# Moving output transposes and a ranking step within a hand-written instruction order (gated linear attention, then a two-level mixture of experts)

## The chip, the cores and the metric

The kernel runs on one core of one Trainium2 chip. The metric is device time in microseconds of one execution; the figure for the kernel before is the median of three runs. An engine name stands for its instruction queue: PE (TensorE, matrix products and transposes), PEld (its weight loads), DVE (VectorE), ACT (ScalarE), POOL (GpSimd), SP (SyncE, which issues most of the transfers).

## The reference

First comes a gated recurrence over 768 steps for 4 batches and 8 heads of 48 channels, then a mixture of 16 experts in 4 groups, with one expert for each of the 3072 tokens.

```python
f = 1.0 / (1.0 + np.exp(-f_logit))
for t in range(S):
    state = f[:, :, t, :, None] * state + np.einsum('bhd,bhe->bhde', k[:, :, t], v[:, :, t])
    y[:, :, t] = np.einsum('bhd,bhde->bhe', q[:, :, t], state)
x = y.transpose(0, 2, 1, 3).reshape(B * S, H * D)          # 3072 x 384
g_idx = argmax(x @ w_group);  e_idx = argmax(x @ w_expert[g_idx])
out = softmax weight of group * softmax weight of expert * (relu(x @ w1[g, e]) @ w2[g, e])
```

All data are 32-bit floats.

## The kernel before

**Two stages.** The first stage computes the recurrence, the routing logits and each token's rank within its expert. It writes the rows x to a table in DRAM (`x_dram`), with the token's weight and number beside each row. The second stage goes over the experts, gathers each expert's rows from that table, multiplies by w1 and w2, and scatters the result to the output.

**Units.** The first stage works in 12 units: six chunks `c` of 128 tokens by two pairs `s` of batches. Unit `i` has c = i // 2 and s = i % 2. The steps of a unit are generators, and each mention of a letter in a hand-written list advances one of them by one piece. PE, DVE, ACT and SP execute exactly in the order in which the lists issue. POOL alone is ordered by the scheduler.

The letters that matter here, with their lines:

- `l` (load) issues q, k, v and f; `c` (`bounded`, L597) bounds f on DVE; `g` (`gated`) takes an exponential and a logarithm on ACT (L607, L610), two decay products `cs` on PE (L616), and two exponentials of each, `eq` and `kh`, on ACT (L617, L618). It also sends the last row of `eq` to a small tile `ends`, through POOL for units up to 9 (L623).
- `m` (`multiplied`) forms `qh` and `kh` on DVE (L636, L639); `t` (`turned`) transposes them on PE (L650), and ACT copies them to `Tq` and `Tk` (L651).
- `b` (`decayed`) transposes `ends` into the decays of a whole chunk (`gt`, L659), which ACT copies (L660). It acts in odd units only.
- `s` (`scored`) computes scores `ap` on PE (L689, or L704 in the first and last three units) and masks them to `am` on DVE (L692, L707).
- `z` copies half of v for the other rows (ACT, L667).
- `w` (`weighed`) makes the products of the state with q (L742) and then the products for slots, that is masked scores times v (L754, L746), and ACT copies the result to `xT` (L757).
- `n` (`stated`) makes the products `ds` for the new state (L722) and then the state on DVE: sum and product with the decays (L727, L728).
- `d` (`done`) makes the logits: `lT` on PE (L770), the copy `lgT` on ACT (L772), then the transpose `lg` (L775) and a sum on DVE (L776).
- `x` (`listed`) turns the outputs back to rows: eight transposes `x_ps` on PE (L795) and three copies on ACT (L797, L800). Rows of units 0 to 7 are kept in SBUF and sent by SP later, four units at a time (`o`, L810, in units 8 and 9); later units send theirs at the third piece of `x` (L803).
- `r` advances the routing of a finished chunk by one of eight pieces. These are: maxima (L197 to L208, two pieces); rank products `rk` on PE (L213, L215) and an exponential on ACT (L216); ranks and counts on DVE (L221 to L224); tables of positions (`ln`, `val`, L230 to L243, two pieces); the weights, with the write of `meta` to DRAM through POOL (L246 to L256); the table products `tb` on PE (L261) and their sum on DVE (L266). For chunk 3 the fourth piece also ranks the experts and writes the numbers of the two most used ones to `who` (L282 to L300).

A number behind a letter shifts the unit: `x-1` is the previous unit's. The list `EVEN` serves units 4 and 6, `ODD` serves units 3, 5 and 7, and `ORDERS` has lists of its own for units 8 (`NU - 4`) to 12.

**Buffers.** Seven PSUM banks with one tag are handed out to whichever result comes next; a bank is free when its last reader is done. `xT`, `Tq` and `Tk` have two buffers each, `am` has three.

Of the kernel before, what the change touches and what calls it, by code (L numbers as in the profile page):

```python
# [23 lines left out]
def kernel(  # L24
# [374 lines left out]
    def fetch(pool, rows, n, top=N, late=False):  # L399

        w = {"n": n, "pool": pool, "early": top < N, "late": late, "blocks": [(j, min(P, n - j * P)) for j in range((n + P - 1) // P)]}
        w["x"] = pool.tile([P, len(w["blocks"]), RW], FP32, tag="xg", bufs=2 if pool is ep else 6, name="xg")
        for j, m in w["blocks"]:
            nc.gpsimd.indirect_dma_start(out=w["x"][:, j, :], out_offset=None, in_=x_dram[0:1 + top, :], in_offset=bass.IndirectOffsetOnAxis(ap=rows[:, j:j + 1], axis=0))  # L404
        return w
# [124 lines left out]
    with ExitStack() as fast:  # L530
# [31 lines left out]
        NU = len(units)  # L562
# [270 lines left out]
        def advance(gens):  # L833
# [10 lines left out]
            t1 t1 t1 t1 b1 c2 g2 g2 s1 s1 s1 s1 p d0 g2 g2 n0 n1 w1 w1 m2 m2 l4 n1  # L844
            d0 x1 x1 t2 t2 t2 t2 c3 g3 g3 x1 s2 s2 s2 s2 w2 g3 g3 d1 w2 n2 m3 m3 c4 g4 g4""".split()
        BEGUN = 3
        EVEN = "l+2 d-2 n-1 r r r x-1 x-1 t t t t g+1 g+1 x-1 r z s s w s s c+2 d-1 g+2 w g+2 n m+1 m+1".split()
        ODD = "l+2 d-2 r r x-1 x-1 t t t t b n-1 g+1 g+1 x-1 r z s s w s s c+2 d-1 g+2 w g+2 n m+1 m+1 r n".split()
        ORDERS = {
            NU - 4: "l+2 o d-2 n-1 r r r x-1 x-1 t t t t g+1 g+1 x-1 r z s s w s s c+2 d-1 g+2 w g+2 n m+1 m+1".split(),  # L850
            NU - 3: "l+2 o d-2 r r x-1 x-1 t t t t b n-1 r g+1 g+1 x-1 r s s s s c+2 w d-1 g+2 w g+2 n m+1 m+1 r n".split(),
            NU - 2: "d-2 r x-1 x-1 r t t t t g+1 g+1 r 1 x-1 s s s s w d-1 w n m+1 m+1 2 3".split(),
            NU - 1: "d-2 r r n-1 x-1 x-1 t t t t r x-1 r s s s s 4 w b d-1 w r r".split(),
            NU: "d-2 r e d-1 x-1 x-1 d-1 x-1 r r r e e r e r r e r r e r e r r e e e e e".split(),
# [3 lines left out]
        def step(nm, i):  # L858
            if nm == "r":
                advance(routes)  # L860
            elif nm == "e":
                next(first[0], None)
            elif nm == "p":
                next(pad)
            elif nm == "o":
                send_kept(i - (NU - 4))
            elif nm in "1234":
                load_next(*((0, 1), (1, 1), (0, 2), (1, 2))[int(nm) - 1])
            elif nm == "h":
                next(turning)  # L870
            elif 0 <= i < NU:
                if nm == "l":

                    load(i, ("k", "qh"))
                    if i + 1 < NU:
                        load(i + 1, ("f",))
                    load(i, ("v",))
                    return
                if (nm, i) not in steps_of:
                    steps_of[nm, i] = STAGES[nm](i)  # L880
                next(steps_of[nm, i], None)
# [14 lines left out]
        for i in range(BEGUN, NU + 1):  # L896
            if i == BEGUN:
                nc.sync.dma_start(out=x_dram[0:1, 0:DM].rearrange("o (h d) -> o h d", d=D), in_=blank[:, 0:D].unsqueeze(1).broadcast_to((1, H, D)))
                nc.sync.dma_start(out=x_dram[0:1, DM:RW], in_=blank[:, D:D + 2])
            for tok in ORDERS.get(i, ODD if i % 2 else EVEN):  # L900
                step(tok[0], i + int(tok[1:] or 0))
# [62 lines left out]
    for n in range(GE - 1):  # L964
        w = ws[n]
# [105 lines left out]
    with tc.If(more > 0), ExitStack() as late:  # L1071
# [5 lines left out]
        with tc.For_i(0, last, 1) as i:  # L1077
# [14 lines left out]
            w = fetch(ep, row, P, late=True)  # L1092
# [32 lines left out]
```

## Time and profile before

| what | value |
|---|---|
| time before, median of 3 runs (lowest, highest) | 412.93 us (411.81, 413.04) |
| the profiled execution: its time | 417.84 us |
| the profiled execution: its span | 416.0 us |
| granted TensorE clock | 0.994 |
| busy PE / DVE / ACT / POOL | 404.0 / 264.3 / 162.2 / 85.7 us |
| units 3 to 8, from the first cs in unit 3 to the first cs in unit 9 | 40.69 to 103.31 us |
| first weights of the experts issued by SP | 118.23 us |
| second stage runs on PE without pauses | from 164.3 us |

Times inside the span are counted from its start. The chain that ended last is a list of pieces in order of time; each piece is what the next one waited for. "issue" is time in which an engine waited for nothing that the profile shows. A timeline row gives start, duration, engine, line, operation, shapes and count; a bracket at its end names the idle time in front of it and what ended it.

### The profile page before, as it was taken

How to read it: one execution, taken by the hardware profiler on the slowest of the kernel's cores; microseconds unless marked ns; L12 is line 12 of the kernel's file. 1: busy time of each engine (PE TensorE's matmuls, PEld its weight loads, DVE VectorE, ACT ScalarE, POOL GpSimd, SP SyncE). 2: the span in 40 equal slices, each digit the busy share in tenths (PEclk: the TensorE clock that was granted, in tenths of full speed). 3: DMA queues.
4: the chain of work that ended last, by engine and by line, in shares of the span. 5: the costliest groups of instructions: out<-in, count | busy, mean ns of one | idle time of the engine just before them, and what ended most of it. 6: DMA issues, size and time to landing. Idle time of an engine off the chain costs nothing.

```text
span 416.0 us, 10268 instructions
## 1 busy us (share of the span) xinstructions
PE 404.0 (97%) x4143; PEld 371.9 (89%) x4143; DVE 264.3 (64%) x783; ACT 162.2 (39%) x365; POOL 85.7 (21%) x132
## 2 busy tenths in 40 slices
PE   8999999999999997999999999999999999999994
PEld 3888888888888966989999999999999999999992
DVE  6666878787998702440799767485595595584230
ACT  6777878887664211211223122222231232232220
POOL 5000010101040174001041221311321230120230
PEclk9999999999999999999999999999999999999999
DMA  9999987879869499855729467586495596485010
GB/s 191 208 216 197 201 179 147 164 159 289 244 225 378 163 337 345 318 179 184 271 84 335 137 245 265 164 315 208 170 348 169 217 352 200 173 318 162 28 48 24
DMA packets 132146, 88.99 MB, mean 214 GB/s; under 512 B 102582, under 2 KB 122748, under 8 KB 132090
## 3 DMA queue, kind: packets, MB, share of 16 engines
q1 hardware_dynamic: 125666, 75.50, 60.6%
q0 software_dynamic: 5792, 11.92, 9.5%
q10 hardware_dynamic: 632, 0.83, 0.6%
q8 instruction: 35, 0.57, 0.6%
q14 instruction: 21, 0.17, 0.1%
HBM read 78.71 MB, written 9.83 MB: 213 GB/s over the span
## 4 chain that ended last, share of the span: by engine, by line
PE 48%; issue 30%; DMA 9%; POOL 6%; DVE 3%; POOLq 1%; another core or an unknown queue 1%; ACT 1%; SPq 0%; ACTq 0%; DVEq 0%
PE hp L450 12%; PE yo L486 6%; DMA out_dram<-yt,xg 6%; PE yo L471 4%; PE cs L616 4%; POOL out_dram L461 4%; PE ap L704 3%; PE y L746 3%; POOL xg L404 2%; PE x_ps L795 2%; PE tr_q L650 2%; PE tr_k L650 2%; PE y L742 2%; PE ap L689 2%; PE y L754 2%
## 5 line engine op out<-in xcount | busy, mean ns | idle before, releaser
L450 PE MATMUL hp<-xe,w 128*128 128x128 f32 (+14 forms) x864 | 141.3, 323 | 2.6 <-issue 1.8
L450 PEld LDWEIGHTS hp<-xe,w 128*128 128x128 f32 x864 | 137.4, 192 | 4.5 <-issue 2.4
L486 PE MATMUL yo<-h,w 128*128 128x230 f32 (+13 forms) x672 | 115.8, 333 | 0.0
L433 DVE STREAM_TRANSPOSE yr<-yT 32x192 f32<-32x192 f32 (+1 forms) x208 | 70.5, 339 | 70.5 <-ACT yT L487 67.9
L486 PEld LDWEIGHTS yo<-h,w 128*128 128x128 f32 x672 | 113.7, 190 | 0.2
L451 ACT ACTIVATE h<-hp 128x256 f32<-128x256 f32 (+14 forms) x72 | 34.2, 478 | 109.1 <-PE hp L450 100.2
L426 DVE STREAM_TRANSPOSE xe<-xg 32x192 f32<-32x192 f32 (+1 forms) x208 | 69.6, 335 | 8.7 <-PE hp L450 5.8
L461 POOL DMA_INDIRECT out_dram<-yt,xg x32 | 34.5, 1078 | 156.1 <-ACT yt L458 150.5
L487 ACT COPY yT<-yo 128x230 f32<-128x230 f32 (+13 forms) x42 | 13.5, 325 | 80.5 <-PE yo L486 80.5
L404 POOL DMA_INDIRECT xg<-x_dram,rows_p x30 | 29.6, 986 | 51.1 <-DMA out_dram<-yt,xg 25.7
L471 PE MATMUL yo<-w,h 128*128 128x384 f32 x64 | 21.3, 486 | 0.0
L707 DVE TENSOR_TENSOR am<-ap,tri 128x512 f32<-128x512 f32 x24 | 15.1, 688 | 7.3 <-PE ap L704 7.3
L616 PE MATMUL cs<-ld_f,tri 128*128 128x384 f32 x48 | 18.5, 505 | 0.5 <-POOL blank L177 0.3
L471 PEld LDWEIGHTS yo<-w,h 128*128 128x128 f32 x64 | 11.9, 190 | 7.4
L458 ACT ACTIVATE yt<-yr,xg 128x384 f32<-128x384 f32 (+13 forms) x26 | 14.4, 604 | 5.4 <-DVE yr L433 5.4
L623 POOL DMA_DIRECT2D ends<-eq x10 | 5.4, 542 | 52.2 <-ACT eq L617 52.2
L692 DVE TENSOR_TENSOR am<-ap,seen 128x384 f32<-128x384 f32 x24 | 12.2, 551 | 5.5 <-PE ap L689 5.5
L757 ACT COPY xT<-y 128x512 f32<-128x512 f32 x24 | 13.4, 587 | 5.0 <-PE y L746 4.4
L651 ACT COPY Tk<-tr_k 128x512 f32<-128x512 f32 x24 | 15.2, 636 | 0.0
L651 ACT COPY Tq<-tr_q 128x512 f32<-128x512 f32 x24 | 15.0, 625 | 0.4 <-PE tr_q L650 0.3
L441 DVE COPY xe<-xg_ps 128x384 f32<-128x384 f32 (+1 forms) x4 | 2.1, 535 | 20.5 <-remote 9.7
L650 PE MATMUL tr_q<-ident,qh 128*128 128x128 f32 x96 | 14.5, 274 | 0.5 <-issue 0.5
(187 smaller groups left out, 448.4 us busy)
## 6 DMA issues: line engine op xcount, KB each, us to landing
w<-in_moe_w_dram SPq DMA_DIRECT2D x34, 1536.0 KB, 7.2
qh<-in_q_dram SPq DMA_DIRECT2D x12, 384.0 KB, 6.1
ld_k<-in_k_dram SPq DMA_DIRECT2D x12, 384.0 KB, 4.4
v<-in_v_dram SPq DMA_DIRECT2D x12, 384.0 KB, 5.4
ld_f<-in_f_logit_dram SPq DMA_DIRECT2D x11, 384.0 KB, 5.5
x_dram<-x_kept SPq DMA_DIRECT2D x2, 1536.0 KB
x_dram<-x POOLq DMA_DIRECT2D x2, 384.0 KB
x_dram<-x ACTq DMA_DIRECT2D x2, 384.0 KB, 7.4
```

What stands on the lines that cost most here:

```text
L404: nc.gpsimd.indirect_dma_start(out=w["x"][:, j, :], out_offset=None, in_=x_dram[0:1 + top, :], in_offset=bass.IndirectOffsetOnAxis(ap=rows ...
L426: squares(w, lambda n, k_, rk, g, rg: nc.vector.transpose(out=xT[rg, 0:n, k_], in_=x[rk, 0:n, g]))
L433: squares(w, lambda n, k_, rk, g, rg: nc.vector.transpose(out=y[rk, 0:n, g], in_=yT[rg, 0:n, k_]))
L450: nc.tensor.matmul(hp[:, o, :], lhsT=w1[:, ko, (f + o) * P:(f + o + 1) * P], rhs=w["xT"][:, ko, :], start=(ko == 0), stop=(ko == KO - 1))
L451: nc.scalar.activation(h[:, f:f + 2, :], hp, AF.Relu)
L461: sent = nc.gpsimd.indirect_dma_start(out=out, out_offset=bass.IndirectOffsetOnAxis(ap=w["x"][0:m, j, DM + 1:RW].bitcast(U32), axis=0), in ...
L471: nc.tensor.matmul(yp, lhsT=w["h"][:, fo, :], rhs=w2[:, fo, :], start=(fo == 0), stop=(fo == FO - 1))
L486: nc.tensor.matmul(yp, lhsT=w2[:, fo, m * P:(m + 1) * P], rhs=w["h"][:, fo, :], start=(fo == 0), stop=(fo == FO - 1))
L616: nc.tensor.matmul(cs.rearrange("t h d -> t (h d)"), lhsT=tri, rhs=nl[:, b], start=True, stop=True)
L650: nc.tensor.transpose(out=pt[:, a, :], in_=w[nm + "h"][:, b, 2 * a:2 * a + 2, :].rearrange("t r d -> t (r d)"), identity=ident)
L651: nc.scalar.copy(w["T" + nm][:, b], pt)
L707: nc.vector.tensor_tensor(am[:, r], ap[r], tri.unsqueeze(1).broadcast_to((P, HP, P)), OP.mult)
```

## The change

Only the lists of order change, for units 3 to 9.

In units 3 to 8 the pieces `x-1` (outputs of the previous unit turned to rows) move from the place around the transposes `t` to a place behind the logits `d-1`, and with them goes the piece `r` that stood behind them. All of this now stands in front of the second piece of `w`, the products for slots. The bound `c+2` follows it. In odd units that `r` is the rank products, in even units the table products and their sum.

In unit 9 the outputs stay where they are. There, the pieces `b n-1` (decays, and the new state on DVE) move from the place in front of the rank products to behind the piece of the ranking.

```diff
-        EVEN = "l+2 d-2 n-1 r r r x-1 x-1 t t t t g+1 g+1 x-1 r z s s w s s c+2 d-1 g+2 w g+2 n m+1 m+1".split()
-        ODD = "l+2 d-2 r r x-1 x-1 t t t t b n-1 g+1 g+1 x-1 r z s s w s s c+2 d-1 g+2 w g+2 n m+1 m+1 r n".split()
+        EVEN = "l+2 d-2 n-1 r r r t t t t g+1 g+1 z s s w s s d-1 x-1 x-1 x-1 r c+2 g+2 w g+2 n m+1 m+1".split()
+        ODD = "l+2 d-2 r r t t t t b n-1 g+1 g+1 z s s w s s d-1 x-1 x-1 x-1 r c+2 g+2 w g+2 n m+1 m+1 r n".split()
         ORDERS = {
-            NU - 4: "l+2 o d-2 n-1 r r r x-1 x-1 t t t t g+1 g+1 x-1 r z s s w s s c+2 d-1 g+2 w g+2 n m+1 m+1".split(),
-            NU - 3: "l+2 o d-2 r r x-1 x-1 t t t t b n-1 r g+1 g+1 x-1 r s s s s c+2 w d-1 g+2 w g+2 n m+1 m+1 r n".split(),
+            NU - 4: "l+2 o d-2 n-1 r r r t t t t g+1 g+1 z s s w s s d-1 x-1 x-1 x-1 r c+2 g+2 w g+2 n m+1 m+1".split(),
+            NU - 3: "l+2 o d-2 r r x-1 x-1 t t t t r g+1 g+1 x-1 r b n-1 s s s s c+2 w d-1 g+2 w g+2 n m+1 m+1 r n".split(),
```

## The prediction

> **What bounds the kernel now.** I read the page's first part, then the stages one by one.
>
> ```profile
> PE 404.0 (97%) x4143; PEld 371.9 (89%) x4143; DVE 264.3 (64%) x783; ACT 162.2 (39%) x365; POOL 85.7 (21%) x132
> ```
>
> TensorE bounds the span. Its ends are modelled, so the 97% hides short waits. The change touches units 3 to 9, which lie between 38 and 112 us. The table by stretches, cut at the first decay product (cs) of each unit, gives two rows of interest: span of the stretch, then busy time of PE, PEld, DVE, ACT, POOL, clock, DMA share, GB/s.
>
> ```profile
> 71.66:81.88 10.22, 10.21 (x244) 8.61 (x242) 8.73 (x26) 8.41 (x19) 1.30 (x2) 1.00 0.81 162
> 91.79:103.31 11.52, 10.48 (x249) 8.84 (x248) 8.90 (x26) 9.33 (x22) 2.04 (x3) 1.00 1.15 277
> ```
>
> A usual unit is PE-full at 9.9 to 10.2 us; DVE and ACT have 1.3 to 1.8 us of slack. The stretch into unit 9 is 11.52 us. The chain that ended last says why:
>
> ```profile
> 94.37 0.17 DVE meta L254
> 94.54 0.14 DVE table L266
> 94.68 0.43 issue
> 95.11 0.78 POOL x_dram L256
> 95.89 7.01 DMA ends<-eq
> 102.90 0.14 issue
> 103.03 0.20 PE gt L659
> ```
>
> On POOL the 4 KB transfer of the decays (ends) stands behind the routing's write of meta; it starts at 95.89 and lands 7.01 us later, and PE's transpose gt waits. Behind gt on PE stand the rank products and cs; behind it on DVE stand the state's product, the ranking of the early experts and the masks of unit 9. The DVE timeline (start, duration) shows the second:
>
> ```profile
> 101.21 0.55 DVE L727 TENSOR_TENSOR st<-st,ds 128x384 f32<-128x384 f32 x1
> 103.47 0.56 DVE L728 TENSOR_TENSOR st<-st,decays 128x384 f32<-128x384 f32 x1 [1.72 <-ACT decays L660]
> 103.95 0.22 DVE L221 TENSOR_TENSOR pick<-rk,run 128x64 f32<-128x64 f32 x1
> 106.85 2.46 DVE L707 TENSOR_TENSOR am<-ap,tri 128x512 f32<-128x512 f32 x4
> ```
>
> From 103.47 DVE has no idle time until 125.3. In units 9 and 10 it is as full as PE.
>
> The third place is smaller: in each unit the products for slots (y L754) start 0.57 us (lT) plus about 0.2 us after the scores, and reach the second mask before DVE has finished it. Unit 4, mask on DVE, then PE:
>
> ```profile
> 54.78 1.02 DVE L692 TENSOR_TENSOR am<-ap,seen 128x384 f32<-128x384 f32 x2 [0.41 <-PE ap L689]
> ...
> 55.61 0.28 PE L754 MATMUL y<-am,other 128*48 128x64 f32 x4
> 55.72 0.39 PE L754 MATMUL y<-am,v 128*48 128x64 f32 x3
> 55.86 0.26 PE L754 MATMUL y<-am,other 128*48 128x64 f32 x1
> ```
>
> Groups of four start every 0.11 us; the fifth, the first on the second mask, stretches to 55.86, just after the mask ends at 55.80. About 0.1 us is lost.
>
> [...] ends was ready when eq ended at 94.0, yet POOL issued it at 95.89, right behind x_dram. [...] Here the 4 KB took 7.01 us, with 1.5 MB of kept rows sent from 94.15; the trace's value is used. [...] Seven banks turn here, so a moved transpose also moves who waits for which bank.
>
> **The change part by part.** No instruction is added or removed. By the two built programs' orders, eight x_ps transposes per unit (0.87 us of PE) go behind lT, then the rank or table products (rk, tb), then the slots. On ACT the three copies to x_kept go between lgT and the exponential of f. On DVE the table's sum goes behind the masks. SP's order is unchanged; the kept rows are sent where they were, long after the copies. On POOL, in three chunks, ends goes in front of meta.
>
> 1. *gt of unit 9.* Before: from the last four tr_k (101.41) to cs (103.31), 1.90 us. Without gt it is 0.44 (the interval 91.35 to 91.79 in unit 8) + 0.12 for rk = 0.56. gt itself moves behind cs and keeps 0.14. PE gains 1.90 - 0.56 - 0.14 = 1.2 us. Can gt wait there? ends issues about 1.9 us earlier (94.0); even with 7.0 us it lands at 101.0, and PE asks at 101.97 + 1.54 = 103.5. No.
>
> But DVE keeps part. rk starts at 101.87; pick follows 0.33 us later (as at 134.28 and 134.61), at 102.2. Pick to masks is 106.85 - 103.95 = 2.90, so 105.1; then the state's two operations, 0.58 + 0.48: masks at 106.2, 0.65 earlier. PE would reach the slots at 103.65 (ap) + 1.99 + 1.03 + 0.57 = 107.25 and finds the first pair only at 106.2 + 1.25 = 107.45, the second at 108.65. So the stage ends about 0.7 us earlier, not 1.2. ACT now makes decays behind the issue of the next ends, near 105.2; the state's second operation comes at 105.7. The names of the early experts come with DVE, so the weight loads (118.23) start some 0.6 us earlier too.
>
> 2. *Slots.* With 0.87 + 0.2 us more PE work between scores and slots, the second mask is ready: 0.1 us in each of six units, 0.6.
>
> 3. *tb.* cs to tb is 1.46 us (71.50 to 72.96), cs to rk 1.39: 0.07 of waiting for val, three times, 0.2. At its new place val is old.
>
> 4. *gt in units 5 and 7.* tr_k to cs is 0.69 against 0.44 without gt. gt costs 0.14; about 0.1 each is the wait for a bank that DVE frees (0.5 us in three waits in the list). The new bank comes from ACT: 0.2.
>
> 5. *Cover given up.* The x_ps transposes stood between lg and tr_q and gave time to DVE and ACT. tr_k needs kh: DVE in an even unit now ends it at scores + 1.0 (mask) + wait for tb; counted from the unit's start that is 9.9 us, and PE asks 0.44 after the unit's end at 10.0. Slack 0.5. The scores need ACT's four copies: PE takes ds 0.85 + lg 0.25 + tr 1.75 + cs 1.45 = 4.3 us from the end of the slots; ACT takes xT 0.96 + logarithm 0.75 + 1.43 + 0.67 = 3.8. Slack 0.5. In front of xT, ACT now has lgT, the x copies (0.92), in odd units dl (0.27), and the exponential (0.75 to start of the next): it is ready 2.6 us after lT, PE ends the slots after 0.87 + 0.2 + 1.7 = 2.8. I cost it at nothing; bounds are 0 and 0.4 us a unit, 2.4 in all. Below nothing is excluded, since the gains are already in 2 to 4.
>
> Steps 2 to 4 give 1.0; with slacks this thin I take 0.7 of it. Sum: 0.7 + 0.7 = 1.4 us. Behind unit 9, PE has 0.2 to 1 us pauses only up to 164, and these hang on the same chain (ranking, meta at 139.51, gathers from 144.72), so they move along; from 164 on PE runs without a break, so the 1.4 us reaches the end. The profiled run, 417.84 us with a span of 416.0, would become 416.4 and 414.6. It lies 1.2% over the median of 412.93; by the same ratio the median becomes 411.5.
>
> **Rivals.**
>
> *The whole stall comes back.* If DVE's chain in unit 9 is no limit (PE's gaps there are only 0.2 us), step 1 gives 1.2, steps 2 to 4 give 1.0; a 0.53 us pause with no releaser at 56.5 may go too, if it hangs on order. 2.2 to 2.7 us: 410.2 to 410.7. For it: PE is the bound in the page. Against: DVE without idle time from 103.47 to 125.3.
>
> *Nothing much arrives.* The pauses of 0.1 us are pipeline effects that stay, and DVE's 0.65 is eaten by a later landing, for instance the gathers at 144.72 whose transfer has its own load. Gain under 0.5: 412.6. [...] Against: the 1.2 us stall is a plain one.
>
> *Slower: ACT becomes the bound of the units.* At its new place in front of the exponential the x copies push xT, logarithm and T copies back, and the scores wait. Until 0.5 us of lateness PE loses nothing; beyond it each unit pays the excess. At 0.73 us late six units pay 1.4 and the gain is gone; at 0.95 us the time is 1.2 us over before, 414.1. For it: slack of xT is only 0.2 us, and DVE's table sum, held by tb, now stands in front of f's bound, which the exponential waits for. Against: ACT was busy 8.4 us of 10.1, and the copies fall into its waits for lT (1.1 us) and f (0.7 us).
>
> **How the numbers follow.** About 0.3%, 1.24 us here, is what tells a change from none; below 411.7 is faster. Likeliest case 0.46, its own range 410.9 to 412.2, two thirds of it faster. Whole stall 0.22, faster. Nothing 0.18, same. Slower 0.14. Faster 0.31 + 0.22 = 0.53, same 0.15 + 0.18 = 0.33, slower 0.14. The range from 409.9 to 413.6 takes in the first two rivals and the edge of the third.
>
> **What would show it.** Right: gt of unit 9 without a wait for ends; ends in front of x_dram on POOL; stretches of 9.9 to 10.1 us; slots without the pause; masks of unit 9 starting 4.9 us after the end of ohe (5.55 before), with y L746 waiting for DVE. Wrong: ap L689 waiting for ACT Tk, or tr_k for DVE kh, in the six units; idle time of ACT's exponential behind table L266; PE pauses between 104 and 134 that grow by what unit 9 gave.

## The result and the profile after

| | before | changed |
|---|---|---|
| median (lowest, highest), 6 runs each, same chip | 412.49 us (411.81, 413.04) | 410.78 us (410.61, 411.04) |
| ratio, 95% interval | | 0.9961, 0.9948 to 0.9974 |
| profiled execution: time, span | 417.84, 416.0 us | 410.61, 408.8 us |

The change makes the kernel 1.7 us faster (1.1 to 2.1 by the interval). Two later sets on other chips gave 0.9977 (0.9967 to 0.9987) and 0.9967 (0.9960 to 0.9975). The prediction was 411.5 us against a median of 412.93, a ratio of 0.9965. The measured 410.78 lies between the range given to the likeliest case (from 410.9) and that of the rival in which the whole stall comes back (up to 410.7), so the time alone doesn't choose between them; the traces do.

The two profiled spans differ by 7.2 us, and that is not the change. The profile of before has pauses on PE from 158 to 164 us, where the experts' layers begin, and a clock of 0.50 behind them, from 164.9 to 168.3 us; the profile after has neither. At the last rank products of the first stage (`rk` L213), in front of that place, the traces stand at 134.28 and 132.54 us: 1.74 us apart, as the medians are. I compare the traces up to there.

The page's first part after the change:

```profile
PE 401.3 (98%) x4143; PEld 369.6 (90%) x4143; DVE 264.9 (65%) x783; ACT 162.9 (40%) x365; POOL 86.0 (21%) x132
```

The busy time of DVE, ACT and POOL is what it was: only waits have moved. The table by stretches, cut at the first decay product (`cs`) of units 6, 7, 8 and 9 (span of the stretch, then busy PE, PEld, DVE, ACT, POOL, clock, DMA share, GB/s):

```profile
69.92:80.03 10.11, 10.11 (x244) 8.57 (x242) 8.64 (x27) 8.65 (x20) 1.51 (x3) 1.00 0.73 143
80.03:90.00 9.97, 9.97 (x243) 8.64 (x243) 7.68 (x20) 8.38 (x21) 0.51 (x1) 1.00 0.88 177
90.00:100.87 10.87, 10.87 (x256) 9.51 (x255) 8.67 (x26) 9.42 (x23) 2.23 (x4) 1.00 0.99 253
```

The stretch into unit 9 was 11.52 us and is 10.87; its PE column now equals its span. `gt` has moved out of this stretch, behind `cs`, and its row on PE has no wait in front of it:

```profile
102.34 0.23 PE L659 MATMUL gt<-ident,ends 16*128 16x16 f32 x1
```

POOL's timeline shows why the transfer is earlier:

```profile
92.54 0.52 POOL L623 DMA_DIRECT2D ends<-eq  x1 [9.50 <-ACT eq L617]
93.05 0.20 POOL L255 COPY meta<-token 128x4 int32<-128x4 int32 x1
93.57 0.79 POOL L256 DMA_DIRECT2D x_dram<-meta  x1 [0.31 <-POOL meta L255]
```

`ends` goes ahead of `meta`, directly behind ACT's `eq`, at 92.54 instead of 95.89. The prediction had 94.0, the end of `eq` before; `eq` itself now ends at 92.25, since the outputs no longer stand in front of it on PE. It also goes 0.48 us ahead of the kept rows (SP issues them at 93.02; before, at 94.15, 1.74 us ahead of `ends`), and lands in 3.9 us instead of 7.01. PE asks for it at 102.34, about 5.9 us after it has landed.

What limits unit 9 now is in the chain of work that ended last, in the stretch from 85 to 112 us (start, length, what):

```profile
100.90 0.03 PE rk L213
100.93 0.10 PE rk L215 x4
101.06 0.24 DVE pick L221
...
103.89 0.15 DVE who L300
104.04 0.47 DVE st L727
104.51 0.03 issue
104.56 0.04 issue
104.60 0.56 DVE st L728
105.16 2.41 DVE am L707 x4
107.57 0.04 issue
107.61 1.09 PE y L746 x16
```

Between the rank products and the second half of the products for slots, everything on the path is on DVE. In the chain of before the same stretch was the transfer (7.01) and PE.

The slots of unit 4, whose rows of before had a gap at the second mask (PE timeline):

```profile
53.72 0.40 PE L770 MATMUL lT<-xT,gw 128*32 128x128 f32 x8
54.05 1.09 PE L795 MATMUL x_ps<-ident,xT 128*128 128x128 f32 x8
54.98 0.28 PE L261 MATMUL tb<-val,ln 128*128 128x64 bf16 x4
55.19 0.32 PE L754 MATMUL y<-am,v 128*48 128x64 f32 x4
...
55.67 0.28 PE L754 MATMUL y<-am,v 128*48 128x64 f32 x4
```

The fifth group keeps the pace. What the rows also show is the price: `x_ps` to the next product is 0.93 us here (54.05 to 54.98) and was 0.87 in front of `tr_q`.

**A ledger of starts.** PE's ends are modelled, so I work with the differences of starts from one kind of product to the next, from one `lg` to the next. (The eight `x_ps` in the rows above last 1.09 us by their modelled ends, and 0.93 from their start to that of `tb`.) Those of one kind, with the same neighbours, agree within 0.02 us over units and runs, save for pauses of up to 0.7 us that come in `y` L754 or `ds` in some units of some runs, with no releaser. Without these:

| | before | changed |
|---|---|---|
| unit with rank products, `lg` to `lg` | 10.23 | 10.22 |
| `cs` to scores, with `rk` in it before | 1.39 + 0.21 | 1.49 |
| `x_ps` | 0.87 | 0.93 |
| `rk` at its new place | | 0.21 |
| `y` L754 | 1.79 | 1.62 |
| unit with table products, `lg` to `lg` | 10.07 | 9.86 |
| `cs` to scores, with `tb` in it before | 1.48 + 0.22 | 1.39 |
| `x_ps` | 0.87 | 0.93 |
| `tb` at its new place | | 0.21 |
| `y` L754 | 1.79 | 1.62 |
| unit 9, `lg` to `lg` | 12.05 (in a second profile of before: 11.66) | 11.41 |
| unit 10, `lg` to `lg` | 9.82 | 9.83 |

A pair of units gains 0.22 us, three pairs 0.66; unit 9 gains 0.64 or 0.25, by how long `gt` waited. In the first two profiles 0.66 + 0.64 = 1.3, and the rest of 1.74 is pauses: 0.6 in unit 4 of before, 0.12 in unit 5 after.

### The profile page after: what moved, and what is told of

Same layout as the page of the kernel before. It is cut to its first block, busy times and chain, and to the rows that moved or that the text cites. A ratio compares the mean times of both kernels' runs of the same rounds, so it can differ in the third digit from the quotient of the medians.

```text
span 408.8 us, 10274 instructions
## 1 busy us (share of the span) xinstructions
PE 401.3 (98%) x4143; PEld 369.6 (90%) x4143; DVE 264.9 (65%) x783; ACT 162.9 (40%) x365; POOL 86.0 (21%) x132
## 3 DMA queue, kind: packets, MB, share of 16 engines
HBM read 78.71 MB, written 9.83 MB: 217 GB/s over the span
## 4 chain that ended last, share of the span: by engine, by line
PE 52%; issue 30%; DMA 8%; POOL 6%; DVE 2%; POOLq 1%; ACT 0%; SPq 0%; DVEq 0%
PE hp L450 12%; DMA out_dram<-yt,xg 7%; PE yo L486 7%; PE yo L471 4%; PE cs L616 4%; POOL out_dram L461 4%; PE x_ps L795 3%; PE tr_q L650 3%; PE tr_k L650 3%; PE y L746 3%; PE y L754 2%; PE ap L704 2%; PE ap L689 2%; POOL xg L404 2%; PE ds L722 2%
## 5 line engine op out<-in xcount | busy, mean ns | idle before, releaser
L450 PE MATMUL hp<-xe,w 128*128 128x128 f32 (+14 forms) x864 | 138.6, 320 | 0.0
L450 PEld LDWEIGHTS hp<-xe,w 128*128 128x128 f32 x864 | 135.8, 190 | 0.8
L650 PE MATMUL tr_k<-ident,kh 128*128 128x128 f32 x96 | 14.3, 273 | 0.0
```

The source lines that it names most:

```text
L450: nc.tensor.matmul(hp[:, o, :], lhsT=w1[:, ko, (f + o) * P:(f + o + 1) * P], rhs=w["xT"][:, ko, :], start=(ko == 0), stop=(ko == KO - 1))
L650: nc.tensor.transpose(out=pt[:, a, :], in_=w[nm + "h"][:, b, 2 * a:2 * a + 2, :].rearrange("t r d -> t (r d)"), identity=ident)
```

## The experiments

Theory of the prediction: the stall of `gt` ends and DVE keeps about half of its 1.2 us; the slots, the table products and a bank give some tenths a unit. Rivals: the whole stall comes back; or the cover that was given up makes ACT late. The first four ran on a chip where all kernels, the one before too, take about 5 us longer (417.54 us median for before, 67 runs) and scatter more, and the changed kernel was not run beside them; what is said of them rests on their traces up to 134 us, which agree with the others unit by unit. The next four shared a second chip (before 412.07 us, 33 runs), the last three a third (before 412.27 us, 53 runs).

**e1: units 3 to 8 as changed, unit 9 as before.**

```diff
-            NU - 3: "l+2 o d-2 r r x-1 x-1 t t t t r g+1 g+1 x-1 r b n-1 s s s s c+2 w ...
+            NU - 3: "l+2 o d-2 r r x-1 x-1 t t t t b n-1 r g+1 g+1 x-1 r s s s s c+2 w ...
```

(The diff is against the changed kernel; unit 9 has its old list.)

> Half of the change: the lists of units 3 to 8 as in the changed kernel, unit 9 as before (decays and state in front of the rank products). On POOL the small transfer of the decays stands in front of the write of meta, as in the changed kernel. Theory A, the moved place of gt in unit 9 is what frees PE: the units give 1.1 us, gt of unit 9 still waits, so about 411.4. Theory B, the earlier issue of the transfer (about 92.5 against 95.9) is enough by itself: it lands by 99.6 even at 7 us, gt asks near 100.9 and finds it, DVE does the state while PE makes cs, the masks of unit 9 start near 104.7 instead of 105.1, and the time is at or below the changed kernel's, 410.3 to 410.8.

Measured: 416.27 us, ratio 0.9970 (0.9954 to 0.9986). `gt` of unit 9, PE timeline, in its old place and without a bracket for a wait:

```profile
100.73 0.23 PE L659 MATMUL gt<-ident,ends 16*128 16x16 f32 x1
```

On POOL `ends` stands in front of `meta`: that comes from the lists of the units, not from the list of unit 9. Unit 9 is 11.58 us from `lg` to `lg`, against 12.05 with a wait of 1.02 us and 11.41 with the moved order. So the earlier transfer takes the wait away alone, and the moved order is worth 0.17 us beyond it. DVE's timeline has what that is:

```profile
101.79 0.56 DVE L728 TENSOR_TENSOR st<-st,decays 128x384 f32<-128x384 f32 x1 [1.24 <-ACT decays L660]
```

With `gt` on time, the state's product still waits 1.24 us for ACT's copy of the decays, and ranking and masks stand behind it. In the moved order DVE waits 0.86 us instead, for `rk`.

**e2: unit 9 alone changed.**

```diff
-            NU - 3: "l+2 o d-2 r r x-1 x-1 t t t t b n-1 r g+1 g+1 x-1 r s s s s c+2 w ...
+            NU - 3: "l+2 o d-2 r r x-1 x-1 t t t t r g+1 g+1 x-1 r b n-1 s s s s c+2 w ...
```

> The other half: units 3 to 8 as before, unit 9 as in the changed kernel. The transfer of the decays is again issued behind meta, near 95.9, and lands near 102.9; gt, now behind cs, asks near 103.5. Theory of the prediction: 0.7 us gained, 411.8. If the two halves add up, this half's gain and that of the units (1.1 us) make the 1.7 us of the whole. Rival, the gain is all in the earlier transfer: nothing here, 412.5.

Measured: 417.74 us, ratio 1.0002 (0.9981 to 1.0022), which can't tell 0.3 to 0.6 us from nothing. The trace can: `ends` stands behind `meta`, `gt` comes at 103.23 without a wait, and unit 9 is 11.41 us, as in the changed kernel. Either half of the change takes the wait away; only the moved order gets below 11.58.

**e3: products moved, outputs stay** (units 3 to 8; unit 9 as changed). The `r` goes behind `d-1`, the three `x-1` keep their places.

```diff
-        EVEN = "... x-1 x-1 t t t t g+1 g+1 x-1 r z s s w s s c+2 d-1 g+2 w ...
+        EVEN = "... x-1 x-1 t t t t g+1 g+1 x-1 z s s w s s d-1 r c+2 g+2 w ...
```

> In units 3 to 8 only the routing's piece (rank products, or table products and sum) moves behind the logits; the turning of outputs stays in front of the transposes. Unit 9 as in the changed kernel. It puts 0.12 to 0.3 us between scores and slots instead of 1.0 to 1.2. Theory A, 0.1 us of cover is enough for the second mask, and the outputs in their old place cost 0.87 us instead of 1.02: slots at 1.63 to 1.7 us, x_ps at 0.87, 410.0 to 410.5, faster than the changed kernel. Theory B, the 0.87 us of the outputs are needed as cover: slots stay at 1.75 us or more and the time is 411.2 to 411.8.

Measured: 417.0 us, ratio 0.9990 (0.9974 to 1.0006). In the ledger the slots take 1.62 us, as with the outputs moved, and `x_ps` 0.87; the units are 10.18 and 9.82 us, 0.04 shorter than in the changed kernel. So 0.22 us of `rk` or `tb` is cover enough for the second mask, and by the trace the outputs need not have moved for it. The times do not confirm it. By the ledger e3 should be about 0.4 us faster than e1, and it is 0.73 us slower on the same chip (an estimate from the two lists of times: 0.1 to 1.3). A pause of 0.68 us in unit 8 of its trace would account for more than half of this gap only if it came in every execution, which no run shows.

**e4: outputs moved, products stay** (units 3 to 8; unit 9 as changed).

```diff
-        EVEN = "... x-1 x-1 t t t t g+1 g+1 x-1 r z s s w s s c+2 d-1 g+2 w ...
+        EVEN = "... t t t t g+1 g+1 r z s s w s s d-1 x-1 x-1 x-1 c+2 g+2 w ...
```

> The counterpart: in units 3 to 8 the turning of outputs moves behind the logits, the routing's piece stays in front of z. Unit 9 as in the changed kernel. Cover of 0.87 us between scores and slots; the table products again wait for val on DVE, with less time in front of them than before since the outputs are gone. If the outputs alone carry the gain: within 0.3 us of the changed kernel, 410.6 to 411.1. If tb now waits for val in three units (val was ready 0.07 us late before, and PE now comes 0.87 us earlier): 0.9 us in each of units 4, 6 and 8, 413 or more.

Measured: 417.38 us, ratio 0.9992 (0.9978 to 1.0006). In the time this is not told from e3. In the list of PE's waits it is:

```profile
PE tb L261 <- DVE val L243: 0.8, 3, 0.3
```

With `x_ps` no longer in front of `tr_q`, PE reaches the table products 0.87 us earlier in the unit, while `val` comes only 0.64 us earlier. `cs` to `tb` is 1.71 us against 1.48, and the unit 10.29 against 10.07; units with rank products stay at 10.22. Moved without the products, the outputs make a pair of units 0.2 us longer.

**e5 and e6: before and the changed kernel once more.** No edit.

> The kernel before, unchanged, with a profile of its own: a second look at the pause of 0.53 us at 56.5 in unit 4 and at the stretch from 158 to 168. If the pause at 56.5 belongs to the order of that kernel it is there again; if it is chance it is elsewhere or gone, and the units 3 to 8 take 60.9 us from x_ps of unit 3 to x_ps of unit 9 instead of 61.5. gt of unit 9 waits for ends again, about 1 us, and the masks of unit 9 start 5.5 us after ohe. Ratio to before 1.000.

> The changed kernel, unchanged, beside the others on one chip. From its first trace: 0.55 us in the units and 0.65 us in unit 9, with 0.53 us more if the pause at 56.5 belongs to the order of the kernel before. So 1.2 to 1.7 us less than before. If this chip has the pause from 158 to 163 in both kernels, the difference stays the same unless the length of that pause differs.

Measured: 412.15 us (1.0004, 0.9991 to 1.0016) and 410.89 us (0.9977, 0.9967 to 0.9987). The trace of before has no pause in unit 4 and none from 158 to 164 us. Its chain around unit 9, in the stretch from 78 to 112 us:

```profile
94.55 0.78 POOL x_dram L256
95.33 6.72 DMA ends<-eq
102.06 0.14 issue
102.19 0.20 PE gt L659
```

The transfer takes 6.72 us and `gt` waits 0.62 us where it waited 1.02, so here the change can save only 0.25 us in unit 9. With 0.66 of the units that is 0.9; the medians are 1.26 apart, and the interval of e6 (0.5 to 1.4 us) takes in both. The trace of e6 has a unit 9 of 11.41 us and pauses of 0.13 and 0.42 us in the slots of units 3 and 5. The same kernel has such pauses in one profile and not in the next, so I put them down to chance; what makes them is not shown.

**e7: state behind the masks in unit 9** (all else as changed). The state's sum and product on DVE stand behind the four masks.

```diff
-            NU - 3: "... r g+1 g+1 x-1 r b n-1 s s s s c+2 w d-1 ...
+            NU - 3: "... r g+1 g+1 x-1 r b s s s s n-1 c+2 w d-1 ...
```

> The changed kernel, but in unit 9 the state's sum and product with decays stand behind the masks on DVE instead of in front of them. Theory: DVE's order is what keeps the rest of the stall; masks then start 1.1 us earlier, near 104.0, y L746 of unit 9 takes 2.0 us instead of 2.6, and PE is 0.55 us earlier at x_ps of unit 10. Of this 0.2 to 0.55 us reach the last rank products (132.54 in the changed kernel), since the work of DVE up to unit 10 is the same in sum. Rival: DVE is the bound through units 9 and 10, so that what PE gains it waits for in unit 10, nothing at the last rank products.

Measured: 410.69 us, ratio 0.9967 (0.9955 to 0.9979): not told from e6. The masks start at 104.76, 6.01 us after `lg` instead of 7.13, and from `y` L746 to `ds` it is 1.80 us instead of 2.44, so DVE had held it. But the list of PE's waits gains a line:

```profile
PE x_ps L795 <- ACT xT L757: 0.4, 1, 0.4
```

The state now stands in front of the bound `ld_f` L597; ACT's logarithm (L607) waits for that bound, and the copies `xT` stand behind the logarithm. `x_ps` of unit 10 comes 11.31 us after that of unit 9, in the changed kernel 11.40, and by the `lg` of unit 11 nothing is left: units 9 and 10 together take 21.23 us in both.

**e8: the copies to x_kept twice** (units 2 to 7; all else as changed), which adds work to ACT in front of the exponential of f.

```diff
+                for again in range(2 if 2 <= i < KEPT else 1):
                 ...
                     nc.scalar.copy(x[:, b], pt[:, :, :, 0:D])
```

> The changed kernel with each copy of the turned outputs done twice on ACT for units 2 to 7, so 0.92 us more work on ACT in each of units 3 to 8 at the place where the change puts it; nothing else differs. By the prediction's slack of 0.5 us: 0.4 us lost in each of six units, 2.5 us in all. By the trace of the changed kernel (0.4 us of waiting in front of xT and about 0.3 us between the last copy Tk and the scores): 0.2 us a unit, 1.0 to 1.5 us. If ACT's idle time of 1.3 us a unit were all usable: nothing.

Measured: 411.64 us, ratio 0.9991 (0.9982 to 1.0000), 0.75 us over e6. ACT has 18 copies and 3.9 us more, 0.65 us a unit. Units with rank products stay at 10.22 us, those with table products go from 9.86 to 10.10, unit 9 from 11.41 to 11.56: 3 x 0.24 + 0.15 = 0.9 us. In a table unit's PE timeline the first scores stretch and are mixed with the products of the state that follow them:

```profile
92.38 1.02 PE L689 MATMUL ap<-Tq,Tk 48*64 48x128 f32 x26
93.17 0.27 PE L742 MATMUL y<-Tq,st 48*64 48x128 f32 x1
93.22 0.27 PE L689 MATMUL ap<-Tq,Tk 48*64 48x64 f32 x4
```

This fits a wait for the last `Tk`, whose copy on ACT ends at 92.57 (91.89 + 0.68). By this ACT's slack is at least 0.65 us in a unit with rank products and about 0.65 - 0.24 = 0.41 in one with table products.

**e9 to e11: the next step, beside the changed kernel.** e9 is the changed kernel. In e10 the state of unit 9 goes behind the bound too, so that nothing on ACT waits for it. In e11, in addition, the outputs of units 3 to 8 stay in their old places, as in e3.

```diff
-            NU - 3: "... r g+1 g+1 x-1 r b n-1 s s s s c+2 w d-1 ...
+            NU - 3: "... r g+1 g+1 x-1 r b s s s s c+2 n-1 w d-1 ...
```

> The changed kernel once more, as the yardstick of the next two on the same chip. From the ledger of starts on PE: a unit with the rank products 10.22 us and a unit with the table products 9.86 us, from one logits product (lg) to the next, 0.16 to 0.34 us more where a pause in y L754 comes by chance; unit 9 from lg to lg 11.41 us. Against the kernel before: three pairs of units at 0.21 us each (10.23 + 10.07 before) and 0.25 to 0.65 us in unit 9, by how late the decays of unit 9 land: 0.9 to 1.3 us faster.

> The changed kernel with the state's product with decays in unit 9 moved once more, behind the four masks and behind the bound of the forget logits (ld_f L597), which ACT's logarithm L607 and behind it the copies xT wait for. Theory A, the order on DVE is the limit of unit 9: masks start at once behind the ranking, y L746 takes 1.97 us in place of 2.61, ACT's xT is no longer late as it was with the state between masks and bound, the x_ps of unit 10 waits for nothing, unit 9 is 10.76 us from lg to lg and 0.6 us of it are at the end too: 0.6 us faster than the changed kernel. Theory B, the sum of the work on DVE is the limit, because it has no idle time from 101 to 123 us: the masks of unit 10 start where they did (115.44 in the changed kernel), its y L746 waits for them, and at most 0.2 us is left at the rank products of unit 11.

> As the run before, but in units 3 to 8 the outputs are turned where they were, in front of tr_q, and only the rank or table products go behind the logits. By the ledger of the run with the products moved alone, units of 10.18 and 9.82 us in place of 10.22 and 9.86: 0.04 us a unit, 0.24 us in six, beyond what the run before gives, if no pause comes by chance. The transfer of the decays goes behind meta again on POOL, but gt, behind cs, asks for it at some 1.5 us later: no wait. With A above 0.8 us faster than the changed kernel, with B 0.2 to 0.4.

Measured: 410.88 us (0.9967, 0.9960 to 0.9975), 410.87 us (0.9967, 0.9959 to 0.9976) and 411.15 us (0.9974, 0.9965 to 0.9984). Neither e10 nor e11 is faster than the changed kernel. In e10 unit 9 is 10.76 us, 0.65 shorter, as theory A said, and unit 10 is 10.47 us, 0.64 longer: theory B. The masks of unit 10 start 17.48 us after the `lg` of unit 9 (115.58 - 98.10), and 17.49 in the changed kernel (115.44 - 97.95). The chain of e10 shows a path without PE in it:

```profile
104.04 0.16 DVE who L300
104.19 2.38 DVE am L707 x4
106.58 0.47 DVE ld_f L597
107.05 0.47 DVE st L727
...
108.17 0.87 DVE qh L636
109.04 0.87 DVE kh L639
...
110.64 0.69 DVE ln L236
111.33 0.47 DVE st L727
```

PE gives the gain back in two places of unit 10: `cs` to `tb` is 1.66 us instead of 1.29, since `val` is late (0.21 us is listed as a wait), and `y` L746 takes 2.22 us instead of 1.93, since its masks are no earlier. In e11 four of six units are the predicted 10.18 and 9.82 us; pauses of 0.49 and 0.12 us in the other two eat the 0.24. All thirteen profiles agree with theory B: units 9 and 10 together end 3.75 us behind the start of the masks of unit 10 in every one, from 21.87 and 18.12 us after the `lg` of unit 9 in the first profile of before to 21.22 and 17.48 in e10. Whether e11's units are better by a measurable amount stays open; neither its time nor that of e3 shows it.

## Why the prediction was right

The total was right: 1.4 us forecast, 1.7 measured, and 0.95, 1.26 and 1.39 us in later sets (the ratio of e6 on its before, and the medians of e6 on e5 and of e9 on its before). The mechanism of unit 9 was right, and its size right for the profile it was read from. The parts of the units were not all right, and it was luck that their errors cancelled.

1. *gt of unit 9* (predicted 0.7 of a stall of 1.2 us, DVE keeping the rest): 0.64, and 0.25 against the second profile of before, where `gt` waits less. Masks were to start 4.9 us after the end of `ohe`, and do: 105.08 - 100.20. `y` L746 waits for DVE, as said. That DVE sets the length is shown by the runs together:

| run | wait of gt | DVE idle in front of state or ranking | masks after lg | unit 9 |
|---|---|---|---|---|
| before | 1.02 | 1.72 | 7.79 | 12.05 |
| before again (e5) | 0.62 | 1.31 | 7.40 | 11.66 |
| early transfer alone (e1) | 0 | 1.24 | 7.32 | 11.58 |
| moved order alone (e2) | 0 | 0.87 | 7.13 | 11.41 |
| changed | 0 | 0.86 | 7.13 | 11.41 |
| state behind the bound (e10) | 0 | 0.87 | 6.01 | 10.76 |

Down to 7.13, unit 9 is 4.26 to 4.28 us longer than the start of its masks: it follows DVE alone. Between e5 and e1 PE's wait falls by 0.62 us and the unit by 0.08. The rival "the whole stall comes back" failed on this. What the prediction had not separated: the new order of unit 9 was not needed for the wait to go (e1), and the transfer was not only issued earlier, by 3.35 us and not 1.9, but took 3.9 us, ahead of the kept rows.

2. *Slots* (predicted 0.1 us in six units): 0.17 in six, 1.0 us. Undersized, since it was read off the one stretched group (55.86 against 55.80), not off the whole of `y` from its start to that of `ds`.

3. *Table products* (predicted 0.07 of wait, three times): 0.19, three times. PE timeline of before, units 6 and 10:

```profile
71.50 1.46 PE L616 MATMUL cs<-ld_f,tri 128*128 128x384 f32 x4
72.96 0.29 PE L261 MATMUL tb<-val,ln 128*128 128x64 bf16 x4
...
113.92 1.46 PE L616 MATMUL cs<-ld_f,tri 128*128 128x384 f32 x4
115.21 0.28 PE L261 MATMUL tb<-val,ln 128*128 128x64 bf16 x4
```

In unit 10 `val` is ready 0.34 us before `tb` starts, and `cs` to `tb` is 1.29 us; in unit 6 `tb` starts 0.06 us after the end of `val`, and it is 1.46 (1.48 in most profiles). The prediction compared with `cs` to `rk`, 1.39, but those units have `gt` in front of `cs`, which adds 0.10: in the changed kernel `cs` to scores is 1.49 us with `gt` and 1.39 without.

4. *A bank for gt in units 5 and 7* (predicted 0.2): nothing. From `tr_q` to `gt` it is 1.84 us and from `gt` to `cs` 0.16 in both kernels. What failed is the reading of the list: the waits named there are those of PEld, gt's weight load, and these lie under running products. In the changed kernel the load waits as long (0.5 us in three), and the list names no engine for it.

5. *Cover given up* (predicted at nothing, slack 0.5 us): right for ACT, whose slack e8 puts at about 0.41 and at least 0.65. The rival "slower" would have needed copies that are late by more than that, and they were not. PE's list has no wait of `tr_k` for `kh` in units 3 to 8 either.

The missing term was the price of the moved products at their new places: the sum took it as what they cost before. `x_ps` takes 0.93 us in front of `rk` or `tb` (1.02 in front of the slots in e4) and 0.87 in front of `tr_q`; `rk` cost 1.39 + 0.21 - 1.49 = 0.11 between `cs` and the scores, and 0.21 behind `x_ps`; `tb` cost 1.29 + 0.22 - 1.39 = 0.12 there without its wait, and 0.21 now. In six, three and three units this takes back 0.36 + 0.30 + 0.27 = 0.93 us. So 1.02 + 0.57 - 0.93 = 0.66 for steps 2 to 5, which is what three pairs of units gain. The discount from 1.0 to 0.7 was argued from thin slacks; it came out at the right number for a wrong reason.

Two statements about the rest of the span were wrong. The pauses of 158 to 164 us do not hang on the first stage: they are in the first profile of before and in those of e1 to e4, and in none of the other eight (the first of the changed kernel, e5 to e11), the kernel before among both. And the 1.2% between the profiled time of before and its median was no scale of the whole execution: it sits at that one place. The first profile of before is 0.81 us behind that of e5 from 134 to 159.7 us, and 6.18 us from 170 us to the end. The ratio of 1.4 to 416 us carried over to the median all the same, since a gain of 1.4 us changes by 0.02 us under it.

## What to carry to other kernels

When a wait of the busiest engine goes away, ask which engine was next behind the same event, and count that engine's queue from the event to the next hand-over; here a wait of 1.02 us was worth 0.64 us, and in the next profile one of 0.62 us was worth 0.25. A gain in one unit has to be followed into the next: moving work within DVE's queue shortened unit 9 by 0.65 us and lengthened unit 10 by 0.64, because the sum of DVE's work over the two units, not its order, was the limit. To price a move on PE, take differences of starts at the old place and at the new one, with the same neighbours on both sides of a comparison, because the same products cost 0.06 to 0.1 us more or less by what stands next to them.

## What the runs showed of the hardware

**A pause of 5 us that is not the kernel's.** The profiles of e1 to e4, and the first profile of before, have PE pauses of 0.2 to 1.5 us in `hp` L450 between 158 and 164 us. The table by stretches, for the profile of before:

```profile
158.00:164.00 6.00, 3.70 (x26) 2.97 (x24) 0.72 (x2) 1.16 (x4) 2.96 (x3) 1.00 1.02 336
164.90:168.30 3.40, 3.40 (x11) 2.97 (x10) 3.29 (x9) 0.00 (x0) 0.00 (x0) 0.50 1.03 401
```

and for the same kernel in e5:

```profile
158.00:164.00 6.00, 6.00 (x41) 5.91 (x40) 3.84 (x12) 1.32 (x3) 2.16 (x3) 1.00 1.00 346
164.90:168.30 3.40, 3.40 (x20) 3.33 (x19) 0.87 (x4) 0.97 (x2) 0.00 (x0) 1.00 1.08 402
```

The same program does 41 products in the six microseconds or 26, with the same DMA share (1.00 and 1.02). The clock behind the pauses is 0.50 for 3.4 us in this profile of before; by the mean clock of longer stretches it is about 3.4 us in e1, e2 and e4 too, and about 6.8 in e3 (estimates). No single pause is longer than 1.5 us. In the profile of before PE was busy for 0.75 us from 160 to 162 us and for 0.97 us from 162 to 164, and the clock was 1.00 in both; it fell at 164.9, when PE had run without a pause from 164.32. What lowers the clock is not shown. What holds PE in the pauses is put down to nothing that the profile shows ("issue" for most of it), and stays open. The medians of before on the chips with and without it are 417.5 and 412 us, a difference of three times what this change does, so times are compared only within a set of runs on one chip, and traces only in front of that place.

**The landing time of 4 KB follows what is in front of it.** In unit 9 `ends` took 3.6 to 4.2 us where it was issued 0.3 to 0.6 us ahead of the 1.5 MB of kept rows (the changed kernel, e6, e7, e9, e10), and 6.7 to 7.4 us where it was issued 1.3 to 1.7 us behind them (before, e5, e11). The five transfers of `ends` that the changed kernel issued from 42.7 to 82.5 us, with no kept rows on their way, took 3.7 to 4.2 us. In the three late cases it also stood right behind the write of `meta` on POOL; which of the two makes it late is not shown.
